# First gate weights on ACT's queue, block 0 normalised ahead of block 1's steps, its gate products in two parts

## The chip, the core and the metric

The kernel runs on one core of a Trainium2 chip. The metric is the device time of one execution in microseconds. The engines are named as in the profile: PE (TensorE, matmuls) with PEld (its weight loads), DVE (VectorE), ACT (ScalarE), POOL (GpSimd) and SP (SyncE, which issues most DMAs).

## The reference

The input x has 2048 tokens of 512 numbers. It is layer-normalised once, and the result `xn` feeds two branches whose outputs are added to x:

```python
xn = _layernorm(x)
return x + _A_ref(xn, A_wqkv, A_wo) + _B_ref(xn, B_w_in, B_w_sp, B_b_sp, B_w_out)

# A: attention, 32 heads of 16, each token sees itself and the 255 before it
scores = einsum('bhqd,bhkd->bhqk', q, k) * Dh ** (-0.5)
p = softmax(where(mask, scores, -1e9))
o = einsum('bhqk,bhkd->bhqd', p, v)  # then @ wo

# B: a gated block mixed over tokens, Fh = 688
z = gelu(einsum('bsd,df->bsf', x, w_in))          # 1376 columns
z1 = z[..., :Fh]
z2 = layernorm(z[..., Fh:])
g = einsum('ts,bsf->btf', w_sp, z2) + b_sp[None, :, None]
return einsum('bsf,fd->bsd', z1 * g, w_out)
```

## The kernel before

The 2048 tokens are 16 blocks of 128. The order on every engine is the order in which the Python program issues instructions; nothing reorders them, and each engine's queue is worked off in that order. Waits between engines are semaphores that the tile framework puts in.

Everything that the change touches lies in the first stage, which lasts to about 58 us and computes `xn`, its transpose `xnT`, the gate products `z` and some of the first q, k and v. For one block the steps are:

- a DMA loads x (`load_block` for blocks 0 to 3, `load_x` for pairs of later ones), on SP's queue;
- `stats(n)`: DVE sums (`bn_stats`, L259) and aggregates them (`bn_aggr`, L260), adds a small number to the variance (`rpow`, L119), and POOL raises it to the power -1/2 (L120);
- `norm(n)`: DVE subtracts the mean and multiplies by that power (L265), which gives `xn`;
- `transpose_x(n)`: four PE transposes into PSUM (L279), and one ACT copy from there to `xnT` (L282). From block 6 on a DMA does the transpose instead (L270);
- `do_z(n, half)`: eight matmuls (four chunks of 128 rows, each in 512 and 176 columns, L290) and a GELU on ACT (L298). Half 1 is the one that is normalised later, half 0 the gate's other factor.

The program order at the start is `warm_up(10)`, `stats(0)`, two loads, `stats(1)`, `norm(0)`, `transpose_x(0)`, `warm_up(3)`, `norm(1)`, `transpose_x(1)`, `do_z(0, 1)`, `stats(2)`, `norm(2)`, `stats(3)`, more loads, `do_z(1, 1)`, `transpose_x(2)`, `stats(4)`, `norm(3)`, `do_z(0, 0)`, and then a loop over n from 2 on that transposes block n + 1 (while that is below 6), does half 1 of block n and half 0 of block n - 1, and keeps `stats` three blocks and `norm` two blocks ahead. From n = 5 it also issues projections of q, k and v between them.

`warm_up` issues matmuls on a tile `zeros` (L251) whose results nothing reads. They run while PE would wait. The first ACT instruction is a table load with a tiny GELU (`warm`, L221). POOL prepares an identity matrix, masks (`fmask`, `esel`, L223 to L231) and one zeroed part of a weight tile (L235) before its first power. One-element memsets by DVE into a tile that a load is about to fill (L318, L332) hold that load back until DVE gets there.

The gate weights `w_in_sb` are four loads (`load_win(half, c0, c1)`, L207), all on SP's queue between the loads of x.

After this stage an order written out by hand (`ORDER`) interleaves the scores, the attention values, the token mix and the output. The change does not touch it.

Of the kernel before, what the change touches and what calls it, by code (L numbers as in the profile page):

```python
# [8 lines left out]
P = 128  # L9
BF = mybir.dt.bfloat16  # L10
F32 = mybir.dt.float32
# [8 lines left out]
FH = 688  # L20
FQ = FH // 2
NB = S_TOK // P
NDC = D // P
# [8 lines left out]
X_DMA = 6  # L32
LAST = 128
ONB = 4
N_WARM = (10, 3)

# [30 lines left out]
def kernel(  # L69
# [12 lines left out]
    nc = tc.nc  # L82
# [6 lines left out]
    xnT = pers.tile([P, NDC, S_TOK], BF, name="xnT")  # L89
# [18 lines left out]
    ps_s = ctx.enter_context(tc.tile_pool(name="ps_s", bufs=3, space=bass.MemoryType.PSUM))  # L108
    ps_y = ctx.enter_context(tc.tile_pool(name="ps_y", bufs=1, space=bass.MemoryType.PSUM))
    ps_g = ctx.enter_context(tc.tile_pool(name="ps_g", bufs=1, space=bass.MemoryType.PSUM))  # L110
    sml = ctx.enter_context(tc.tile_pool(name="sml", bufs=3))
# [5 lines left out]
    def rpow(dst, var, n):  # L117
        v = sml.tile([P, NB], F32, name="rs_v")
        nc.vector.tensor_scalar(out=v[:, :n], in0=var, scalar1=LN_EPS, scalar2=None, op0=ALU.add)  # L119
        nc.gpsimd.tensor_tensor(out=dst, in0=v[:, :n], in1=negh[:, :n], op=ALU.pow)  # L120
# [57 lines left out]
    with tc.tile_pool(name="win_pool", bufs=1) as winp, tc.tile_pool(  # L178
        name="xsp", bufs=8
    ) as xsp, tc.tile_pool(name="xnp", bufs=4) as xnp:  # L180
        w_in_sb = winp.tile([P, NDC, F], BF, name="w_in_sb")
        zeros = winp.tile([P, 512], BF, name="zeros")
        nc.vector.memset(zeros[:], 0.0)  # L183
        nc.vector.memset(fmask[:], 1.0)
        nc.vector.memset(esel[:], 1.0)
        make_identity(nc, ident[:])
        xs_tiles = {}
# [3 lines left out]
        def load_block(n):  # L191
            if n % 2 == 0:
                xs_pairs[n // 2] = xsp.tile([P, 2, D], BF, name="xs")
            xs_tiles[n] = xs_pairs[n // 2][:, n % 2, :]
            nc.sync.dma_start(out=xs_tiles[n], in_=x2[n * P : (n + 1) * P, :])
# [7 lines left out]
            for j in range(2):  # L203
                xs_tiles[2 * n2 + j] = xs[:, j, :]

        def load_win(half, c0, c1):
            nc.sync.dma_start(  # L207
                out=w_in_sb[:, c0:c1, half * FH : (half + 1) * FH],
                in_=B_w_in[c0 * P : c1 * P, half * FH : (half + 1) * FH].rearrange(
                    "(c p) f -> p c f", p=P  # L210
                ),
            )

        load_block(0)
        load_block(1)
        load_win(1, 0, 2)
        load_block(2)
        load_win(1, 2, 4)
        load_block(3)
        warm = sml.tile([P, 1], F32, name="warm")  # L220
# [3 lines left out]
            out=fmask[:], in_=fmask[:], pattern=[[-1, P]], compare_op=ALU.is_gt,  # L224
# [3 lines left out]
            out=esel[:], in_=esel[:], pattern=[[-32, 4]], compare_op=ALU.is_ge,  # L228
# [3 lines left out]
            out=esel[:], in_=esel[:], pattern=[[32, 4]], compare_op=ALU.is_ge,  # L232
# [15 lines left out]
        def warm_up(n):  # L248
            wt = ps_s.tile([P, 2, 512], F32, name="warm_t", tag="S")
            for i in range(n):  # L250
                nc.tensor.matmul(  # L251
                    wt[:, 0, :], lhsT=zeros[:, 0:P], rhs=zeros[:], start=True, stop=True
                )

        xn_tiles = {}

        def stats(n):
            st = sml.tile([P, nc.vector.BN_STATS_DIM], F32, name="st")
            nc.vector.bn_stats(out=st[:], in_=xs_tiles[n])  # L259
            nc.vector.bn_aggr(out=mvx[:, n, :], in_=st[:])  # L260
            rpow(rstdx[:, n : n + 1], mvx[:, n, 1:2], 1)

        def norm(n):
            xn = xnp.tile([P, D], BF, name="xn")
            nc.vector.tensor_scalar(  # L265
                out=xn[:], in0=xs_tiles[n], scalar1=mvx[:, n, 0:1],
                scalar2=rstdx[:, n : n + 1], op0=ALU.subtract, op1=ALU.mult,
            )
            if n >= X_DMA:
                nc.sync.dma_start_transpose(out=xnT[:, :, n * P : (n + 1) * P], in_=xn[:])  # L270
            else:
                xn_tiles[n] = xn

        def transpose_x(n):
            xn = xn_tiles.pop(n)
            pool, tag = (ps_y, "y") if n == 1 else (ps_g, "g")
            tp = pool.tile([P, NDC, P], BF, name="tp", tag=tag)
            for c in range(NDC):
                nc.tensor.transpose(  # L279
                    out=tp[:, c, :], in_=xn[:, c * P : (c + 1) * P], identity=ident[:]  # L280
                )
            nc.scalar.copy(out=xnT[:, :, n * P : (n + 1) * P], in_=tp[:])  # L282

        def do_z(n, half):
            zp2 = ps_s.tile([P, 2, 512], F32, name="zs", tag="S")
            zp = zp2[:].rearrange("p a q -> p (a q)")
            f0 = half * FH
            for c in range(NDC):
                for lo, hi in Z_RANGES:
                    nc.tensor.matmul(  # L290
                        zp[:, lo:hi],
                        lhsT=xnT[:, c, n * P : (n + 1) * P],
                        rhs=w_in_sb[:, c, f0 + lo : f0 + hi],
                        start=(c == 0),
                        stop=(c == NDC - 1),
                    )
            dst = z1_all if half == 0 else z2_all
            nc.scalar.activation(out=dst[:, n, 0:FH], in_=zp[:, 0:FH], func=ACT.Gelu_apprx_tanh)  # L298

# [14 lines left out]
        early = [(kind, 0, grp) for grp in range(3) for kind in "kqv"]  # L314

        warm_up(N_WARM[0])
        stats(0)
        nc.vector.memset(w_in_sb[0:1, 0, 0:1], 0.0)  # L318
        load_x(2)
        load_win(0, 0, 2)  # L320
        load_win(0, 2, 4)
        stats(1)
        norm(0)
        transpose_x(0)
        warm_up(N_WARM[1])
        norm(1)
        transpose_x(1)
        do_z(0, 1)
        stats(2)
        norm(2)  # L330
        stats(3)
# [3 lines left out]
        for n2 in range(4, NB // 2):  # L335
            load_x(n2)
        do_z(1, 1)
        transpose_x(2)
        stats(4)
        norm(3)  # L340
        do_z(0, 0)
        nc.vector.tensor_reduce(
            out=emask[:, 0:1], in_=esel[:], op=ALU.add, axis=mybir.AxisListType.X
        )
        nc.vector.tensor_scalar(
            out=emask[:, 1:2], in0=emask[:, 0:1], scalar1=-1.0, scalar2=1.0,
# [232 lines left out]
    def finish():  # L579
# [9 lines left out]
        out=w_out_sb[:, 0:5, :], in_=B_w_out[0:640, :].rearrange("(c p) n -> p c n", p=P)  # L589
# [52 lines left out]
```

## Time and profile before

| what | value |
|---|---|
| median of 3 runs | 265.3 us (265.15 to 265.53) |
| the profiled execution | 265.24 us |
| its span, first to last instruction | 263.5 us |
| PE busy | 256.9 us, 98% of the span |
| ACT busy | 205.5 us, 78% |
| DVE busy | 197.9 us, 75% |
| POOL busy | 122.0 us, 46% |
| x block 0, issued and landed | 0.81 and 2.95 us |
| x block 1, issued and landed | 1.27 and 3.46 us |
| first gate weights, issued and landed | 1.73 and 5.03 us |
| second gate weights, issued and landed | 2.71 and 6.38 us |
| QKV weights, issued and landed | 9.42 and 15.78 us |

A line of the timeline gives start and duration in us, engine, line, operation, what it writes and reads, shapes, how many instructions were merged, and in brackets the idle time of the engine before it and what ended that. A busy engine is one that has an instruction in flight; matmuls overlap, so two that start 0.22 us apart may each be listed with 0.38 us. The chain of waits is followed back from the last instruction, at each step to what released it.

### The profile page before, as it was taken

How to read it: one execution, taken by the hardware profiler on the slowest of the kernel's cores; microseconds unless marked ns; L12 is line 12 of the kernel's file. 1: busy time of each engine (PE TensorE's matmuls, PEld its weight loads, DVE VectorE, ACT ScalarE, POOL GpSimd, SP SyncE). 2: the span in 40 equal slices, each digit the busy share in tenths (PEclk: the TensorE clock that was granted, in tenths of full speed). 3: DMA queues.
4: the chain of work that ended last, by engine and by line, in shares of the span. 5: the costliest groups of instructions: out<-in, count | busy, mean ns of one | idle time of the engine just before them, and what ended most of it. 6: DMA issues, size and time to landing. Idle time of an engine off the chain costs nothing.

```text
span 263.5 us, 7433 instructions
## 1 busy us (share of the span) xinstructions
PE 256.9 (98%) x3166; PEld 143.4 (54%) x3199; DVE 197.9 (75%) x384; ACT 205.5 (78%) x233; POOL 122.0 (46%) x140
## 2 busy tenths in 40 slices
PE   8999999999999999999999999999999999999995
PEld 3665665654546465555565456655564454545542
DVE  5899999667786888788797778897869563786542
ACT  2777767699999999999988989988898996782000
POOL 4334446116542573768553556455468453355100
PEclk9999999999999999999999999999999999999999
DMA  7892233940505073130360322661329263636432
GB/s 215 277 301 42 42 56 68 166 161 2 109 4 112 7 105 41 43 82 13 69 82 2 80 44 41 76 51 38 82 86 179 59 132 94 140 93 151 107 85 77
DMA packets 61233, 23.83 MB, mean 90 GB/s; under 512 B 52321, under 2 KB 60689, under 8 KB 61201
## 3 DMA queue, kind: packets, MB, share of 16 engines
q1 hardware_dynamic: 60720, 23.06, 41.1%
q8 instruction: 25, 0.41, 0.7%
q10 hardware_dynamic: 432, 0.30, 0.4%
q0 software_dynamic: 48, 0.00, 0.3%
q14 instruction: 8, 0.06, 0.1%
HBM read 8.41 MB, written 2.10 MB: 40 GB/s over the span
## 4 chain that ended last, share of the span: by engine, by line
PE 97%; issue 1%; DVE 1%; DVEq 0%
PE gf L402 31%; PE zs L290 14%; PE S L496 12%; PE m L151 10%; PE o_t L549 8%; PE fo L439 8%; PE m L135 6%; PE fo L433 5%; PE warm_t L251 2%; PE tp L279 1%; DVE xnT L444 0%; DVE o_c L565 0%; DVE zeros L183 0%; DVEq L565 0%
## 5 line engine op out<-in xcount | busy, mean ns | idle before, releaser
L504 ACT ACTIVATE E<-S 128x1024 bf16<-128x1024 f32 x180 | 168.9, 1042 | 16.9 <-PE S L496 9.1
L402 PE MATMUL gf<-z_all,wspT 128*128 128x344 bf16 x512 | 95.1, 311 | 0.1
L515 POOL TENSOR_SCALAR_AFFINE_SELECT E<-E 128x1024 bf16<-128x1024 bf16 x64 | 79.3, 1262 | 31.3 <-ACT E L504 31.1
L402 PEld LDWEIGHTS <-wspT 128*128 128x128 bf16 x512 | 44.1, 98 | 35.9 <-issue 15.4
L520 DVE TENSOR_TENSOR E<-E,fmask 128x1024 bf16<-128x1024 bf16 x56 | 53.0, 973 | 2.4 <-ACT E L504 2.3
L571 POOL TENSOR_TENSOR o_norm<-o_c,rsum 128x256 bf16<-128x256 f32 x32 | 21.5, 672 | 61.9 <-DVE rsum L569 59.2
L290 PE MATMUL zs<-w_in_sb,xnT 128*128 128x512 bf16 (+1 forms) x249 | 39.1, 307 | 0.4
L496 PE MATMUL S<-q_ring,k 32*128 32x128 bf16 (+2 forms) x760 | 37.2, 267 | 0.0
L298 ACT ACTIVATE z_all<-zs 128x688 bf16<-128x688 f32 x32 | 23.8, 744 | 12.5 <-PE zs L290 12.5
L151 PE MATMUL m<-xnT,wqkv 128*128 128x512 bf16 x111 | 31.5, 380 | 1.0 <-issue 0.2
L290 PEld LDWEIGHTS <-xnT 128*128 128x128 bf16 x256 | 22.2, 98 | 14.9
L409 DVE SCALAR_TENSOR_TENSOR z_all<-gf,b_all,z_all 128x344 bf16<-128x344 f32 x32 | 18.1, 567 | 14.6 <-PE gf L402 14.6
L565 DVE STREAM_TRANSPOSE o_c<-o_t 128x512 f32<-128x512 f32 x32 | 22.3, 698 | 7.2 <-PE o_t L549 6.5
L496 PEld LDWEIGHTS <-k 32*128 32x128 bf16 x760 | 12.7, 92 | 25.9 <-issue 25.2
L444 DVE TENSOR_TENSOR xnT<-fo,xnT 128x512 bf16<-128x512 f32 (+2 forms) x17 | 11.2, 659 | 17.0 <-PE fo L439 15.3
L549 PE MATMUL o_t<-E,v 128*32 128x128 bf16 (+1 forms) x1080 | 23.4, 238 | 0.0
L439 PE MATMUL fo<-w_out_sb,uT 128*128 128x512 bf16 (+2 forms) x101 | 23.3, 366 | 0.1
L549 PEld LDWEIGHTS <-v 128*32 128x32 bf16 x1080 | 19.2, 97 | 5.1 <-issue 4.6
L171 DVE TENSOR_TENSOR k<-m,emask 128x1024 bf16<-128x1024 f32 x13 | 15.8, 1218 | 3.1 <-PE m L151 3.0
L120 POOL TENSOR_TENSOR rstdx<-rs_v,negh 128x1 f32<-128x1 f32 x16 | 10.2, 640 | 17.0 <-DVE rs_v L119 14.5
L151 PEld LDWEIGHTS <-wqkv 128*128 128x128 bf16 x128 | 11.7, 98 | 11.6 <-issue 1.7
L135 PE MATMUL m<-wqkv,xnT 128*128 128x128 bf16 x256 | 16.9, 219 | 0.2 <-DVE o_c L565 0.2
(51 smaller groups left out, 174.6 us busy)
## 6 DMA issues: line engine op xcount, KB each, us to landing
xnT<-in_A_x_dram SPq DMA_DIRECT2D x4, 512.0 KB, 4.6
out_dram<-xnT SPq DMA_DIRECT2D x13, 128.0 KB, 1.8
xs<-in_A_x_dram SPq DMA_DIRECT2D x6, 256.0 KB, 6.8
wqkv<-in_A_wqkv_dram SPq DMA_DIRECT2D x1, 1536.0 KB, 6.4
w_in_sb<-in_B_w_in_dram SPq DMA_DIRECT2D x4, 344.0 KB, 4.2
w_out_sb<-in_B_w_out_dram SPq DMA_DIRECT2D x1, 640.0 KB, 6.1
xs<-in_A_x_dram SPq DMA_DIRECT2D x4, 128.0 KB, 2.7
wo_sb<-in_A_wo_dram SPq DMA_DIRECT2D x1, 512.0 KB, 4.9
```

Of the source, the lines that this page charges most:

```text
L135: nc.tensor.matmul(m[:, j * P : (j + 1) * P], lhsT=xnT[:, c, n * P : (n + 1) * P], rhs=wqkv[:, c, 2 * D + G * P : 2 * D + (G + 1) * P], st ...
L151: nc.tensor.matmul(m, lhsT=wqkv[:, c, w0 : w0 + P], rhs=xnT[:, c, grp * 512 : (grp + 1) * 512], start=(c == 0), stop=(c == NDC - 1),)
L290: nc.tensor.matmul(zp[:, lo:hi], lhsT=xnT[:, c, n * P : (n + 1) * P], rhs=w_in_sb[:, c, f0 + lo : f0 + hi], start=(c == 0), stop=(c == NDC ...
L298: nc.scalar.activation(out=dst[:, n, 0:FH], in_=zp[:, 0:FH], func=ACT.Gelu_apprx_tanh)
L402: nc.tensor.matmul(gf[:, 0:FQ], lhsT=wsp_tiles[n][:, c, :], rhs=z2_all[:, c, lo : lo + FQ], start=(c == 0), stop=(c == NB - 1),)
L439: nc.tensor.matmul(fo[:, c0:c1], lhsT=uT_tiles[n][:, c, :], rhs=w_out_sb[:, c, c0:c1], start=False, stop=(c == NFC - 1),)
L496: nc.tensor.matmul(S[:, h2, j * P : (j + w) * P], lhsT=k_t[(G, kb // 4)][32 * s : 32 * s + 32, e, (kb % 4) * P : (kb % 4 + 1) * P], rhs=q_ ...
L504: nc.scalar.activation(out=E[:, j : j + 3 : 2, 0:nb, :].rearrange("p h b c -> p h (b c)"), in_=tiles[pr][:, :, 0 : nb * P], func=ACT.Exp, ...
L515: nc.gpsimd.affine_select(out=E[:, :, j, :], in_=E[:, :, j, :], pattern=[[0, 8], [1, P]], compare_op=ALU.is_ge, fill=0.0, base=0, channel_ ...
L520: nc.vector.tensor_tensor(out=E[:, :, j, :], in0=E[:, :, j, :], in1=fmask[:].unsqueeze(1).to_broadcast([P, 8, P]), op=ALU.mult,)
L549: nc.tensor.matmul(T[32 * s : 32 * s + 32, e, j * P : (j + l) * P], lhsT=v_t[(G, kb // 4)][:, kb % 4, s, e : e + 2, :].rearrange("p a d -> ...
L565: nc.vector.transpose(out=C[:, 0 : 32 * DH], in_=Tb)
```

## The change

There are six edits, all at the start:

- `load_win` takes a queue, and the first load of the gate weights (half 1, chunks 0 and 1) goes to ACT's queue, ahead of ACT's table load. A one-element memset of DVE into its target comes before it.
- The dummy matmuls read a constant one that exists from the start, in place of a tile that DVE zeroes. The second group has two, not three.
- `sums(n)` is the first instruction of `stats(n)`, split off, so that it can be issued alone. Block 1's sums stay ahead of `norm(0)`; its aggregate, add and power come after `norm(0)`, `transpose_x(0)` and the second dummies.
- The copy of block 0's transposes is cut in two: ACT copies chunks 0 and 1, DVE copies 2 and 3.
- `do_z(0, 1)` is issued as chunks 0 and 1, then `transpose_x(1)`, then chunks 2 and 3.
- `norm(3)` comes after block 4's sums alone, and the rest of `stats(4)` after `norm(3)`.

```diff
-N_WARM = (10, 3)
+N_WARM = (10, 2)
...
-        zeros = winp.tile([P, 512], BF, name="zeros")
-        nc.vector.memset(zeros[:], 0.0)
+        ones_w = nc.const_aps.tensor(1.0, [P, P], BF)
+        ones_m = nc.const_aps.tensor(1.0, [P, 512], BF)
...
-        def load_win(half, c0, c1):
-            nc.sync.dma_start(
+        def load_win(half, c0, c1, queue=nc.sync):
+            queue.dma_start(
...
         load_block(0)
         load_block(1)
-        load_win(1, 0, 2)
+        nc.vector.memset(w_in_sb[0:1, 0, FH : FH + 1], 0.0)
+        load_win(1, 0, 2, nc.scalar)
         load_block(2)
...
-                    wt[:, 0, :], lhsT=zeros[:, 0:P], rhs=zeros[:], start=True, stop=True
+                    wt[:, 0, :], lhsT=ones_w, rhs=ones_m, start=True, stop=True
...
+        st_tiles = {}
+
+        def sums(n):
+            st_tiles[n] = sml.tile([P, nc.vector.BN_STATS_DIM], F32, name="st")
+            nc.vector.bn_stats(out=st_tiles[n][:], in_=xs_tiles[n])
+
         def stats(n):
-            st = sml.tile([P, nc.vector.BN_STATS_DIM], F32, name="st")
-            nc.vector.bn_stats(out=st[:], in_=xs_tiles[n])
+            if n not in st_tiles:
+                sums(n)
+            st = st_tiles.pop(n)
             nc.vector.bn_aggr(out=mvx[:, n, :], in_=st[:])
...
-            nc.scalar.copy(out=xnT[:, :, n * P : (n + 1) * P], in_=tp[:])
-
-        def do_z(n, half):
-            zp2 = ps_s.tile([P, 2, 512], F32, name="zs", tag="S")
-            zp = zp2[:].rearrange("p a q -> p (a q)")
+            dst = xnT[:, :, n * P : (n + 1) * P]
+            if n == 0:
+                nc.scalar.copy(out=dst[:, 0:2, :], in_=tp[:, 0:2, :])
+                nc.vector.tensor_copy(out=dst[:, 2:4, :], in_=tp[:, 2:4, :])
+            else:
+                nc.scalar.copy(out=dst, in_=tp[:])
+
+        zp_open = {}
+
+        def do_z(n, half, c0=0, c1=NDC):
+            if c0 == 0:
+                zp_open[n] = ps_s.tile([P, 2, 512], F32, name="zs", tag="S")
+            zp = zp_open[n][:].rearrange("p a q -> p (a q)")
             f0 = half * FH
-            for c in range(NDC):
+            for c in range(c0, c1):
...
+            if c1 < NDC:
+                return
             dst = z1_all if half == 0 else z2_all
...
-        stats(1)
+        sums(1)
         norm(0)
         transpose_x(0)
         warm_up(N_WARM[1])
+        stats(1)
         norm(1)
+        do_z(0, 1, 0, 2)
         transpose_x(1)
-        do_z(0, 1)
+        do_z(0, 1, 2, NDC)
         stats(2)
...
         transpose_x(2)
+        sums(4)
+        norm(3)
         stats(4)
-        norm(3)
         do_z(0, 0)
```

## The prediction

> **What bounds the kernel now.** I read the page's chain of waits first, then the same chain in order of time at the start of the span, then the timeline of the first 14 us on every engine, because every edit lies there.
>
> ```profile
> span 263.5 us, 7433 instructions
> ...
> PE 97%; issue 1%; DVE 1%; DVEq 0%
> ```
>
> TensorE is 97% of the chain that ends last. The idle times before its matmuls show why: after 11 us the largest in the whole timeline is 0.19 us. Nothing downstream can absorb a delay or give a gain back, so whatever TensorE loses or wins before it settles into block 2's products is lost or won at the end. The chain at the start:
>
> ```profile
> 1.26 4.45 PE warm_t L251 x10
> 5.71 0.43 PE tp L279 x4
> 6.13 0.72 PE warm_t L251 x3
> 6.85 0.22 PE tp L279 x4
> 7.08 2.33 PE zs L290 x16
> 9.41 0.22 PE tp L279 x4
> 9.63 1.17 PE zs L290 x8
> 10.80 0.37 PE tp L279 x4
> ```
>
> TensorE never stops here, but the first three rows are fill: the dummy matmuls cover the time until block 0 and block 1 are normalised. Real work without a break starts with the four transposes of block 1. Only the last row holds a stall (0.37 us for transposes that take 0.22 us, for block 3's normalised tile). What feeds TensorE is one serial chain on VectorE and GpSimd, in the timeline:
>
> ```profile
> 2.98 0.69 DVE L259 BATCH_NORM_STATS2 st<-xs 128x6 f32<-128x512 bf16 x1 [1.62 <-DMA xs<-in_A_x_dram]
> ...
> 4.16 0.56 POOL L120 TENSOR_TENSOR rstdx<-rs_v,negh 128x1 f32<-128x1 f32 x1 [0.87 <-DVE w_in_sb L318]
> ...
> 5.01 0.41 DVE L265 TENSOR_SCALAR xn<-xs,mvx,rstdx 128x512 bf16<-128x512 bf16 x1
> ...
> 5.87 0.41 DVE L265 TENSOR_SCALAR xn<-xs,mvx,rstdx 128x512 bf16<-128x512 bf16 x1 [0.46 <-POOL rstdx L120]
> ...
> 6.17 0.59 ACT L282 COPY xnT<-tp 128x512 bf16<-128x512 bf16 x1 [3.87 <-PE tp L279]
> ...
> 6.92 0.18 DVE L260 BATCH_NORM_AGGREGATE mvx<-st 128x2 f32<-128x6 f32 x1
> ...
> 7.95 0.41 DVE L265 TENSOR_SCALAR xn<-xs,mvx,rstdx 128x512 bf16<-128x512 bf16 x1 [0.66 <-POOL rstdx L120]
> ```
>
> Blocks 0 and 1 are normalised at 5.01 and 5.87, 0.86 apart, because block 1's power on GpSimd (5.17) runs while block 0 is normalised. Block 2 shows the undisturbed cost: from its aggregate (6.92) to its normalising (7.95) is 1.03 us.
>
> **Part one, block 0 ahead of block 1's steps.** Block 1's aggregate and add leave the place before block 0's normalising. That now starts when its power ends, 4.16 + 0.56 + 0.02 = 4.74, so 0.27 us earlier. Its transposes follow 0.49 later as before (5.01 to 5.50): 5.23. The dummies are out of the way, since they need no zeroed tile any more; the constant one they read now is set by GpSimd at 0.36, before the start barrier that lets ScalarE and GpSimd go at 0.80. They start about 0.84 instead of 1.26, ten at the 0.43 spacing of the timeline, done at 5.1.
>
> **Part two, the split copy.** In the changed kernel as built, VectorE's half of block 0's copy waits for a semaphore of ScalarE, not of TensorE: it runs behind ScalarE's half. VectorE works in order, and behind this copy are queued block 1's aggregate, add and normalising; GpSimd's power for block 1 waits for that add, and TensorE's transposes of block 1 for the normalising. So block 1's steps, which ran beside block 0's, come after block 0's whole trip:
>
> - ScalarE's half starts 0.67 after the transposes (5.50 to 6.17): 5.90. Its length is not in the trace; 744 ns at 688 columns and 586 at 512 make 0.9 ns a column, so 0.36 (bounds 0.20, its one-column row, and 0.59): 6.26.
> - VectorE's half: 0.69 for a 512-column PSUM cast and 0.29 for a 128-column add out of PSUM make 0.42 for 256, less the 0.08 by which VectorE starts its next instruction ahead (bounds 0.2 and 0.69): the aggregate starts at 6.63.
> - Plus block 2's 1.03: block 1 is normalised at 7.66, where it was 5.87.
>
> TensorE's first four products of block 0 fill only 0.58 us of this (half of 1.17). The dummy that was dropped lies in the same hole: even two at the slow spacing end at 6.5, the products by 7.1 at full clock or 7.7 at the slow one. If block 1 came early the dummies would cost 0.2; here they cost nothing.
>
> **What is late next.** Block 1's transposes at 7.66 + 0.46 (10.31 to 10.77 for block 3) = 8.12. Their copy starts 0.42 later (6.69 to 7.11) and takes 0.59: 9.13, so block 1's products start near 9.2; they started at 8.08. That is 1.1 us. VectorE then runs block 2 (2.08 after block 1, 5.87 to 7.95) at 9.74, in time for its transposes at 9.2 + 1.17 = 10.37. Block 3 is not in time. It followed block 2 by 2.36 (7.95 to 10.31); the edit that lets only block 4's sums stand before it makes that 2.07 (sums 9.30 + 0.69, power done at 10.00). So 9.74 + 2.07 = 11.81, and transposes at 12.27, where TensorE is free at 11.76 and where they stood at 10.77. The delay is 1.50 us. Block 4 then has cover: normalised near 13.7, plus 0.46 is 14.2, needed at 12.27 + 2.57 = 14.84.
>
> The loads behind these steps move too. The fence for the QKV weights (9.31) waits about 1.8 us longer; they landed at 15.8 and were first used at 19.6, and both ends shift by nearly the same.
>
> **Part three, weights through ACT's queue.** SP's later loads issue about 0.46 earlier (one issue, 1.73 to 2.19) and none of them was waited for. ScalarE pays: it waits for VectorE's new fence (about 1.13), issues for about 0.43, and only then loads its table (1.28) and runs its warm-up (0.20), ending near 3.1 instead of 2.3. GpSimd's two small selects and the 0.53 us memset stand behind that warm-up; they end near 4.09, and block 0's power is wanted at 4.16. Taken at nothing, with 0.07 us of cover; past that every bit is paid by all blocks.
>
> The 344 KB now start near 2.2 us, beside the first two blocks of x.
>
> ```profile
> 2.00:3.00 1.00, 1.00 (x4) 0.35 (x3) 0.03 (x1) 0.29 (x2) 0.57 (x3) 1.00 0.96 247
> ```
>
> This is the window from 2 to 3 us: busy time of TensorE, its weight loads, VectorE, ScalarE and GpSimd, then the granted clock, the DMA engines' share and GB/s. At 0.96 they are full already. Block 0 landed at 2.95 and opens the chain; block 1 landed at 3.46 and has until 3.98. A gain is excluded: neither load is issued sooner. The upper bound is block 1 sharing all its time: 3.46 - 2.29 = 1.17 us becomes up to twice that, 4.6 us, 0.6 too late; an even share for the part in which the weights are there gives 0 to 0.35. I take 0.2, nearer to the lower end because block 0's packets were mostly out by 2.45. The Trainium skill ("DMA: Bandwidth & Descriptors", issuing engines are not separate DMA queues) says that DMAs of different engines share the same 16 DMA engines and interleave, so that spreading them saves issue time alone; by it this delay is above zero, and by independent queues it would be zero and the sum 0.2 us less.
>
> **Sum.** 1.50 + 0.20 = 1.70 us on the profiled execution's own 265.24 (span 263.5 and 1.74 around it; the median of the runs is 265.3): 266.9 us. With the lower bounds (halves about 0.15 shorter each, no contention, and the clock up before block 0's transposes, whose 0.67 to the copy then becomes the 0.42 of block 1) the delay is 0.95: 266.2. With VectorE's copy at its upper bound (+0.27) and contention at 0.35 it is 2.1: 267.4.
>
> **Rivals.**
> - Faster: the reorder wins and the wait behind the copy is hidden. Block 0's products start at 6.36 instead of 6.91, block 3's stall goes: 0.55 + 0.14 = 0.69, 264.6 us. It needs block 1 normalised by about 6.4, and VectorE's order speaks against it by 1.2 us. Chance 0.04.
> - No change to be measured (0.2%, 0.53 us either way): most of the delay is absorbed by early x or cheap copies. Needs both halves and the power to shrink well under their rows. 0.03.
> - Slower still, by GpSimd: if ScalarE's issue and table load end 0.1 to 0.5 later than reckoned, block 0's power is late by that less 0.07; 267.3 to 267.6. It decides from an issue that ends after 1.70. 0.12.
> - The clock falls back: TensorE idles from about 7 to 8.1. The dummies of before ran at the slow 0.43 spacing from 1.26 to about 6.1; a second such spell of 4.9 us at half speed costs 2.4: 269.3. Against it: a 1.1 us hole is short beside 4.9. 0.03. The Trainium skill ("TensorE: Matmul & The Clock Gate", Part 1) closes the gate only after a whole idle window of about 3.4 us; by it, this doesn't happen.
>
> The forecast itself has 0.78, with 266.2 to 267.4. The range adds the GpSimd case: 266.1 to 267.6. Faster 0.04, within 0.2% 0.03, slower 0.93.
>
> **What would show it.** VectorE's copy starting after ScalarE's half ends; block 1's aggregate behind it near 6.6 and its normalising near 7.7; an idle stretch of about a microsecond on TensorE before block 1's transposes; a second near 12 before block 3's; from there TensorE's rows as before, 1.5 to 1.9 us later. Block 1 normalised before 6.5 would make the forecast wrong, and block 0 normalised after 5.1 would put a share on loads or GpSimd.

## The result, and the profile after

The changed kernel takes 267.15 us (median of 5 runs, 266.83 to 267.5), the kernel before in the same series 265.48 us (265.15 to 265.77). The ratio is 1.0062, with a 95% interval of 1.0048 to 1.0076: slower by 1.67 us. The profiled execution is the one of 267.15 us (span 265.4 us), 1.91 us above the profiled one of before (265.24 us). Forecast was 266.9 us.

The engines' share of the chain of waits, from the page of the changed kernel:

```profile
PE 93%; DVE 2%; DMA 1%; issue 1%; POOL 1%; SPq 0%; ACT 0%; DVEq 0%
```

TensorE carried 97% of the chain before. The lost share has gone to a stretch at the start, which the chain in order of time spells out (start, length, what):

```profile
1.27 3.67 DMA xs<-in_A_x_dram
...
4.96 0.69 DVE st L262
5.66 0.32 DVE xn L273
...
6.03 0.41 PE tp L287 x4
...
6.46 0.38 ACT xnT L292
...
6.87 0.29 DVE xnT L293
7.16 0.10 DVE mvx L268
...
8.11 0.41 DVE xn L273
...
12.28 0.42 DVE xn L273
...
12.75 0.40 PE tp L287 x4
```

Before, this stretch was TensorE's own: dummies to 5.71, then real work with one stall. Now the chain runs through every other engine until 12.75, block 3's transposes. Two things in it are new. It begins with block 1's load of x, landed at 4.94 (before: 3.46). And it goes through both halves of block 0's copy (6.46 and 6.87) ahead of block 1's aggregate. TensorE's idle times say the same, in the timeline:

```profile
6.03 0.40 PE L287 MATMUL tp<-ident,xn 128*128 128x128 bf16 x4 [0.76 <-DVE xn L273]
8.58 0.40 PE L287 MATMUL tp<-ident,xn 128*128 128x128 bf16 x4 [0.93 <-DVE xn L273]
12.75 0.40 PE L287 MATMUL tp<-ident,xn 128*128 128x128 bf16 x4 [0.36 <-DVE xn L273]
```

Block 3's transposes stood at 10.77 before, so they are 1.98 us late. Everything after them follows at that distance: TensorE's last matmul starts at 261.99, where it started at 260.01.

The late x is the surprise. The DMA queues between 2.50 and 3.25 us, of before first and then of the changed kernel (q1 is SP's queue, q10 ACT's; packets, MB, share of the 16 DMA engines):

```profile
DMA packets 185, 0.18 MB, mean 245 GB/s; under 512 B 21, under 2 KB 185, under 8 KB 185
...
q1 hardware_dynamic: 185, 0.18, 97.5%
```

```profile
DMA packets 76, 0.09 MB, mean 119 GB/s; under 512 B 8, under 2 KB 76, under 8 KB 76
...
q10 hardware_dynamic: 56, 0.08, 57.6%
q1 hardware_dynamic: 20, 0.01, 9.9%
```

SP's queue, which carries block 1 of x, falls from 185 packets to 20, and the 16 engines together move half as much. The 185 of before also hold 45 packets of the weights, which went by SP's queue there; of x itself (packets of 1024 bytes) 119 went before and 12 in the changed kernel. The weights do not merely take a share: their first packets are slow. In the DMA records single weight packets take up to 0.70 us (0.06 us later on), and x nearly stands still meanwhile. That x's packets wait behind them on the same engines would explain it but isn't shown, as the records don't say which engine moved a packet. Before, the weights started as slowly (up to 0.59 us), but behind both blocks of x on the same queue. From 3.25 us on the engines are full again in the changed kernel and packets of the two queues alternate, too late for block 1. The weights landed at 5.14 us (before: 5.03), so the earlier issue won nothing for them either.

### The profile page after: what moved, and what is told of

It is laid out like the page before. It is cut to its first block, busy times and chain, and to the rows that moved or that the text cites. A ratio compares the mean times of both kernels' runs of the same rounds, so it can differ in the third digit from the quotient of the medians.

```text
span 265.4 us, 7432 instructions
## 1 busy us (share of the span) xinstructions
PE 257.1 (97%) x3165; PEld 142.9 (54%) x3198; DVE 197.9 (75%) x385; ACT 205.4 (77%) x233; POOL 121.7 (46%) x140
## 4 chain that ended last, share of the span: by engine, by line
PE 93%; DVE 2%; DMA 1%; issue 1%; POOL 1%; SPq 0%; ACT 0%; DVEq 0%
PE gf L423 31%; PE zs L306 13%; PE S L517 12%; PE m L151 10%; PE o_t L570 8%; PE fo L460 8%; PE m L135 6%; PE fo L454 5%; DMA xs<-in_A_x_dram 1%; DVE st L262 1%; POOL rstdx L120 1%; DVE xn L273 1%; PE tp L287 0%; DVE xnT L465 0%; DVE o_c L586 0%
```

## The experiments

Each kernel was timed beside the kernel before. Theory A in the expectations is the forecast's mechanism with a higher price on the load: block 1's steps wait for its x and then for block 0's copy. Theory G is that idle stretches on TensorE cost clock. The other rivals are in the texts. Diffs are against the changed kernel unless said otherwise. "Start shift" is how much later than before the first-stage rows stand once they follow at a constant distance (before: block 3's transposes at 10.77, block 4's at 13.34); block 3's own time is given where it helps.

### e1: first weights back on SP's queue

```diff
-        nc.vector.memset(w_in_sb[0:1, 0, FH : FH + 1], 0.0)
-        load_win(1, 0, 2, nc.scalar)
+        load_win(1, 0, 2)
```

> The changed kernel with the first gate weights back on SP's queue; the rest of the change stays. Theory A (two costs in series on VectorE's chain: block 1's x lands 1.5 us later because the weights share the DMA engines, which moves block 0's normalising from 4.74 to 5.58, and block 1's aggregate and add stand behind the copy): block 1's x lands near 3.5 again, block 0 is normalised near 4.75, block 1 near 7.5, block 3's transposes start near 12.2 (12.75 in the changed kernel, 10.77 before): 0.3 to 0.6 us below the changed kernel, about 1.2 above before. Rival B (the loads are the whole cost): back at before, within 0.2 us. Rival C (the order behind the copy is the whole cost): no difference from the changed kernel.

Measured: 266.36 us (266.12 to 266.56), before 265.37; ratio 1.0034 (1.0021 to 1.0047). The chain in order of time, block 0's half copies and what follows:

```profile
5.93 0.38 ACT xnT L291
...
6.34 0.29 DVE xnT L292
...
7.58 0.41 DVE xn L272
...
12.21 0.40 PE tp L286 x4
```

Block 1 of x landed at 3.37, block 0 was normalised at 4.86. The start shift is 1.44 us: the wait behind the copy alone, and within 0.06 of the forecast's 12.27 for block 3. So the load is worth 1.97 - 1.44 = 0.53 us in the shift and 0.68 us in the medians' differences (1.67 and 0.99). Rivals B and C are both out: the time is neither that of before nor that of the changed kernel.

### e2: only the load through ACT's queue, in the kernel before

Against the kernel before:

```diff
+        nc.vector.memset(fmask[:], 1.0)
+        nc.vector.memset(w_in_sb[0:1, 0, FH : FH + 1], 0.0)
         nc.vector.memset(zeros[:], 0.0)
-        nc.vector.memset(fmask[:], 1.0)
...
-        load_win(1, 0, 2)
+        load_win(1, 0, 2, nc.scalar)
```

Two memsets now stand ahead of the zeros that the dummies read, so the dummies start at 1.44 us, where it was 1.26.

> The kernel before with only its first gate weights on ACT's queue (and the one-element fence memset for that). Theory A: block 1's x lands near 4.9, its sums start there, and since in this order aggregate and add of block 1 also stand ahead of block 0's normalising, that comes near 6.0 instead of 5.01; every later row moves by the same, 0.9 to 1.0 us above before. Rival B (the loads are the whole cost): as slow as the changed kernel, 1.6 to 1.9 above before. Rival C: no difference from before.

Measured: 266.08 us (265.8 to 267.59, 10 runs), ratio 1.0036 (1.0021 to 1.005): +0.71. Two of the ten took 267.49 and 267.59, and the first of these is the profiled one. Its timeline shows why:

```profile
7.23 1.49 PE L252 MATMUL warm_t<-zeros 128*128 128x512 bf16 x3
...
8.51 0.63 PE L280 MATMUL tp<-ident,xn 128*128 128x128 bf16 x4
```

Three dummies take 1.49 us where they took 0.93 before, and the transposes 0.63 where full speed makes it 0.39: TensorE ran at half speed until 10.17 us, where it came to full speed at 6.15 before. It had idled for 0.94 us before block 0's transposes, as block 1 of x landed at 5.33 and its sums stand ahead of block 0's normalising. So the load alone costs about 0.7 us in the median: more than the 0.2 I took, less than the 0.9 to 1.0 expected here (e5 has the reason), and far from Rival B's 1.6. In some executions a late clock comes on top.

### e3: block 1's aggregate, add and power issued ahead of block 0's transposes and copy

```diff
         norm(0)
+        stats(1)
         transpose_x(0)
         warm_up(N_WARM[1])
-        stats(1)
         norm(1)
```

> The changed kernel with block 1's aggregate and add issued before block 0's transposes, so that VectorE's half copy stands behind them and only block 1's normalising behind the copy. Theory A: block 1 is normalised near 7.1 (8.11 in the changed kernel), block 3's transposes start near 11.7, 1.0 us below the changed kernel and 0.8 to 0.9 above before. Rival D (what costs is the wait of VectorE's half for ScalarE's half, whatever stands behind it): the halves stay in series, so less than 0.3 us below the changed kernel. Rival B: no difference from the changed kernel.

Measured: 266.2 us (266.07 to 266.5), ratio 1.0032 (1.002 to 1.0044); start shift 1.04. The load is left as in the changed kernel, the copy too. VectorE's rows:

```profile
6.00 0.17 DVE L268 BATCH_NORM_AGGREGATE mvx<-st 128x2 f32<-128x6 f32 x1
...
6.98 0.29 DVE L293 COPY xnT<-tp 128x256 bf16<-128x256 bf16 x1 [0.62 <-ACT xnT L292]
...
7.19 0.40 DVE L273 TENSOR_SCALAR xn<-xs,mvx,rstdx 128x512 bf16<-128x512 bf16 x1
```

With the power running beside the copy, block 1 is normalised at 7.19 instead of 8.11, although x is as late as ever. 0.93 us of the start shift is gone, where Rival D allowed less than 0.3. The order of VectorE's queue is a cause by itself.

### e4: block 0's copy whole on ACT

```diff
-            if n == 0:
-                nc.scalar.copy(out=dst[:, 0:2, :], in_=tp[:, 0:2, :])
-                nc.vector.tensor_copy(out=dst[:, 2:4, :], in_=tp[:, 2:4, :])
-            else:
-                nc.scalar.copy(out=dst, in_=tp[:])
+            nc.scalar.copy(out=dst, in_=tp[:])
```

> The changed kernel with the whole of block 0's copy on ScalarE; VectorE has no part in it. Theory A: block 1's aggregate follows block 0's normalising at once (5.9), block 1 is normalised near 6.95, block 3's transposes start near 11.6, 1.1 to 1.2 us below the changed kernel and 0.7 to 0.8 above before (the late load stays). Rival B (loads alone): no difference from the changed kernel. Rival E (block 0's first products are what sets the time, and they start later with a whole copy): slower than the changed kernel by 0.2.

Measured: 266.23 us (265.77 to 267.23, 10 runs), ratio 1.0034 (1.0023 to 1.0045); start shift 1.04, block 1 normalised at 7.18. The same as e3 by another road: it is VectorE's half copy, standing ahead of block 1's steps, that holds them. Two of the ten executions took 267.1 and 267.23; a late clock as in e2 would fit, but no trace of them was kept.

### e5: both undone, the load on SP and the copy on ACT

The edits of e1 and e4 together.

> The changed kernel with both suspected costs taken away: the first gate weights back on SP's queue, and the whole of block 0's copy on ScalarE. Theory A: block 0 is normalised near 4.8, block 1 near 6.2, block 3's transposes start near 10.8, as before (10.77): within 0.2 us of before, either way. If something else in the change costs (the dummies' constant, the products in two parts), it stays 0.3 us or more above before. Rival F (with block 1's aggregate and add still behind block 0's normalising, the rest of the change gains): 0.3 us or more below before.

Measured: 264.99 us (264.85 to 265.4, 11 runs), before 265.29 (23 runs); ratio 0.9989 (0.9981 to 0.9998). The slowdown is gone. TensorE's chain at the start:

```profile
0.84 4.42 PE warm_t L251 x10
...
5.94 0.60 ACT xnT L290
...
6.58 0.76 PE zs L301 x4
7.34 0.24 PE tp L286 x4
```

The start shift is +0.10, so the edits that are left (the early dummies, the order of normalising, the products in two parts, block 4's sums) bring nothing at the start that block 3's transposes would keep. The median is 0.30 us below before, which is Rival F's number, but not for its reason: the 0.3 us come from elsewhere. In the kernel before and in the changed one TensorE waits in the middle for a transpose of VectorE, as in this row of the changed kernel:

```profile
86.58 1.05 PE L135 MATMUL m<-wqkv,xnT 128*128 128x128 bf16 x16 [0.20 <-DVE o_c L586]
```

With what follows it the wait is worth 0.29 us: e5's last matmul starts 0.19 us earlier than that of before (259.82 and 260.01), after a start shift of +0.10. The wait is in the profiles of before, after, e3, e4, e6, e7, e9 and e11 and missing in e1, e2, e5, e8 and e10. This is also part of why e1's median is 0.99 and not 1.44 above before, and e8's 0.74 and not 1.07. What decides it was not found.

### e6: two small edits alone, in the kernel before

Against the kernel before, with `sums` split off as in the change:

```diff
-N_WARM = (10, 3)
+N_WARM = (10, 2)
...
-        stats(4)
-        norm(3)
+        sums(4)
+        norm(3)
+        stats(4)
```

> The kernel before with two edits of the change alone: two dummies in the second group instead of three, and block 3 normalised after block 4's sums alone. Theory A: nothing is put behind a copy and no load moves; block 0's products start near 6.8 instead of 6.91 and block 3's transposes near 10.53 instead of 10.77: 0.2 us below before, at the edge of what can be measured. If the order ahead of block 3's transposes doesn't matter: no difference from before.

Measured: 265.14 us (265.01 to 265.54, 11 runs), ratio 0.9994 (0.9985 to 1.0003): not to be told from no change. In the profiled execution (265.44 us) block 3's transposes stand at 10.97. The chain names a load there (issued at 4.69, landed at 10.35: a part of the other half's weights), not block 3's normalising.

### e7: block 0's products in one piece

```diff
-        do_z(0, 1, 0, 2)
         transpose_x(1)
-        do_z(0, 1, 2, NDC)
+        do_z(0, 1)
```

> The changed kernel with block 0's products in one piece behind block 1's transposes, as before. Theory A (block 3's normalised tile sets TensorE's place, through VectorE): the first four products leave the hole at 6.9, block 1's products start near 9.97 instead of 9.66, and block 3's transposes still near 12.75: no difference from the changed kernel, within 0.15 us. Rival E (TensorE's own work at the start sets the time): 0.3 us above the changed kernel.

A miss: 268.67 us (267.06 to 270.4, 6 runs), ratio 1.0125 (1.009 to 1.016). The profiled execution is the fastest of the six, and its timeline has the expected place for block 3 (12.67), with a longer hole ahead of block 1's transposes:

```profile
5.96 0.40 PE L287 MATMUL tp<-ident,xn 128*128 128x128 bf16 x4 [1.31 <-DVE xn L273]
...
8.51 0.40 PE L287 MATMUL tp<-ident,xn 128*128 128x128 bf16 x4 [1.72 <-DVE xn L273]
```

The two executions at 267.06 and 267.3 had a mean granted clock of 1.00; the others 0.994 (268.36 and 268.99), 0.986 (269.84) and 0.985 (270.4). All five timed executions of the changed kernel had 0.998 or more. So the products that the change puts into the hole (0.76 us of them at 6.89), though they move no row of the chain, seem to keep the clock up there; e9 tests that. The other runs of this series (e5, e6, e8) had 0.998 or more in every execution.

### e8: e2 with three more dummies

Against e2:

```diff
-N_WARM = (10, 3)
+N_WARM = (13, 3)
```

> The run with the ACT queue alone, with 13 dummies in the first group instead of 10, so that TensorE has no hole before block 0's transposes. The profiled execution of that run had its matmuls at 0.43 us spacing until 10 us, and it took 267.49 where the median was 266.08. Theory G (the hole from 5.7 to 6.8 lets the clock come up a whole window late in some executions): no execution above 266.8, median near 266.0. Rival H (the late executions come from the load's landing alone): some executions stay near 267.5.

Measured: 266.03 us (265.92 to 266.63, 5 runs), ratio 1.0032 (1.002 to 1.0044). TensorE has no hole ahead of block 0's transposes (6.54), and none of the five executions is late. Two late in ten against none in five is thin, but the median (+0.74) and the start shift (+1.07) again price the load alone, this time with the clock up in time.

### e9: e7 with nine dummies where it had two

Against e7:

```diff
-N_WARM = (10, 2)
+N_WARM = (10, 9)
```

> The changed kernel with block 0's products in one piece (which alone gave 267.06 to 270.4) and nine dummies in the second group instead of two, so that TensorE has work from block 0's transposes to about 8.2 us. Theory G (in the run without them, the empty stretch from 6.8 to 8.5 makes the clock fall or come up late in most executions): all executions near the changed kernel, 266.9 to 267.6. Rival I (the products in one piece cost by their place in the queue, whatever fills the hole): median above 268 again.

Measured: 267.3 us (267.02 to 268.37, 6 runs), ratio 1.0074 (1.006 to 1.0088). TensorE's rows:

```profile
6.60 2.13 PE L252 MATMUL warm_t<-const-bfloat16-1.0 128*128 128x512 bf16 x9
8.92 0.40 PE L287 MATMUL tp<-ident,xn 128*128 128x128 bf16 x4 [0.19 <-DVE xn L273]
```

The hole of e7 is filled with work that nothing reads, and 1.4 us come back; five of six executions are within 267.02 to 267.48. The one at 268.37 (clock 0.998) may come from the hole before block 0's transposes, which is still there (1.86 us); that wasn't tested.

### e10: e5, with the sums of later blocks in VectorE's waits

Against e5:

```diff
         stats(1)
+        sums(2)
         norm(1)
-        do_z(0, 1, 0, 2)
         transpose_x(1)
-        do_z(0, 1, 2, NDC)
+        do_z(0, 1)
         stats(2)
+        sums(3)
         norm(2)
```

> The run with ScalarE's whole copy and the weights on SP, further with the sums of blocks 2 and 3 ahead of the normalising of blocks 1 and 2 (in VectorE's waits for GpSimd), and block 0's products in one piece behind block 1's transposes. Theory A: block 3 is normalised near 9.3 instead of 10.36 and no longer late, block 1's products start near 8.05 instead of 8.24, block 3's transposes near 10.7 instead of 10.89: 0.1 to 0.2 us below that run. If the landing of the x blocks holds the sums back, no difference.

Measured: 265.03 us (264.75 to 265.54, 12 runs), ratio 0.9984 (0.9975 to 0.9992). It is 0.16% below the kernel before and isn't to be told from e5. Block 2's transposes start at 9.44, e5's at 9.41. Block 3 is normalised at 9.96, where it was 10.31 before, and its transposes wait all the same, until 11.18, for products that wait for weights:

```profile
4.68 5.87 DMA w_in_sb<-in_B_w_in_dram
...
10.60 0.74 PE zs L301 x4
11.34 0.22 PE tp L286 x4
```

This is the load that e6's chain named. Once VectorE's chain is shortened, that landing is what comes next. The start shift is +0.39; the time is no longer because the wait of 0.29 us described at e5 is missing.

### e11: the load on ACT's queue, held until block 0's sums have started

```diff
-        nc.vector.memset(w_in_sb[0:1, 0, FH : FH + 1], 0.0)
-        load_win(1, 0, 2, nc.scalar)
...
         warm_up(N_WARM[0])
+        sums(0)
+        nc.vector.memset(w_in_sb[0:1, 0, FH : FH + 1], 0.0)
+        load_win(1, 0, 2, nc.scalar)
         stats(0)
```

> The changed kernel with the first gate weights still on ACT's queue, but issued behind the warm-up and held back until block 0's sums are taken (near 3.7 us), so that they are not in flight beside blocks 0 and 1 of x. Theory A: block 1's x lands near 3.4, block 0 is normalised near 4.75, block 1 near 7.5, block 3's transposes start near 12.2, as with the weights on SP: about 0.5 us below the changed kernel; the weights land later, near 7, into the hole before block 1's transposes. Rival J (ACT's queue itself delays the loads of x, whenever it is used): block 1's x late as in the changed kernel, no difference from it.

A miss: 270.8 us (269.61 to 272.51, 6 runs), ratio 1.0206 (1.0178 to 1.0234). The side of x does what holding the load was to do: block 1's sums start at 3.99, straight after block 0's steps, block 0 is normalised at 4.75 and block 1 at 7.30. So Rival J is out. But the weights, issued at 3.72 beside what SP had issued before, now come last:

```profile
9.13 1.31 PE L304 MATMUL zs<-w_in_sb,xnT 128*128 128x512 bf16 x4 [3.08 <-DMA w_in_sb<-in_B_w_in_dram]
10.23 0.63 PE L285 MATMUL tp<-ident,xn 128*128 128x128 bf16 x4
```

Four products take 1.31 us (0.76 in the changed kernel). Windows of 2 us (TensorE, its weight loads, VectorE, ScalarE, GpSimd, granted clock, DMA share, GB/s) show the clock itself:

```profile
8.00:10.00 2.00, 0.87 (x3) 0.40 (x3) 1.27 (x5) 0.00 (x0) 0.55 (x1) 0.51 0.90 320
...
12.00:14.00 2.00, 2.00 (x9) 0.93 (x7) 1.90 (x8) 0.74 (x1) 1.06 (x2) 0.50 0.80 237
```

The clock falls at 8.04 us, 1.99 us into the hole of 3.08 us, and TensorE runs at half speed until 14.87 us. Block 3's transposes stand at 15.87, 5.1 us late. The profiled execution loses a further 1.6 us in one place: TensorE idles for 1.54 us before 62.28 us, for a cast of VectorE that stands behind a load of 4 KB (the bias `b_bf`), which landed 14.4 us after its issue where it took 6.0 before. The waiting weights, not x, are the main price of this version.

## Why the prediction was right

The direction, the engine and the mechanism hold, and the total is within the range. Two terms were wrong in size, and partly offset each other, so the closeness of the total is partly luck.

**The wait behind the copy: right, 1.50 forecast, 1.44 measured** (e1, where the load is out of the way). Its steps there and in the forecast: block 0 normalised at 4.86 (4.74), ScalarE's half copy at 5.93 (5.90) for 0.38 (0.36), VectorE's half behind it for 0.29 (0.42, the one size that was clearly off), block 1's aggregate at 6.54 (6.63), its normalising at 7.58 (7.66), block 2's at 9.66 (9.74), block 3's at 11.75 (11.81). VectorE's copy does wait for ScalarE's, and e3 and e4 each take about 0.9 us off the changed kernel by freeing block 1's steps from it. The stall ahead of block 3's transposes, and the cover for block 4, came as worked out.

**The load: the step that failed.** I let block 1 of x be late by "0 to 0.35" and took 0.2, with an upper bound of 4.6 us for its landing. It landed at 4.94, beyond that bound, because I divided bandwidth and the trace shows a near stall: 12 packets of x where 119 went. In the shift this cost 0.53 us (1.97 against e1's 1.44); e2 and e8 give 0.71 and 0.74 in the median for the load alone. The reason given, that block 0's packets "were mostly out by 2.45", was beside the point: block 0 landed at 2.99 (2.95 before), and it was block 1 that stood still. The rule of the Trainium skill ("DMA: Bandwidth & Descriptors", issuing engines are not separate DMA queues) agrees with this trace in that the packets of the two queues alternate and together fill the engines from 3.25 us on (share 1.02). The load of the other queue paid.

**Why the total still came near.** Block 1's sums were 0.85 us late to start (4.96, VectorE idle for 0.85), so block 0 was normalised at 5.58, 0.84 after the forecast's 4.74 and past the 5.1 that the prediction had named as the sign of a share on loads or GpSimd. Of this 0.24 came back because the first transposes ran at full speed and ScalarE followed them after 0.43 instead of 0.67, and 0.13 through VectorE's shorter half copy. Block 3's transposes came at 12.75, where the working with its 0.20 for the load has 12.47. Against the forecast delay of 1.70 the profiled executions differ by 1.91 and the medians by 1.67.

**The two terms don't add up.** Load alone 1.07 (e8), copy alone 1.44 (e1), both 1.97 and not 2.51. The rows account for the gap. Block 1's sums are 0.86 later than in e1 (4.96 and 4.10), in e8 1.06 later than before: 0.20. In e1 block 0's normalising waits for GpSimd's power after those sums, in the changed kernel it follows them at once: 0.14. And from there ScalarE's half copy follows 0.19 sooner, as the first transposes run at full speed.

**The rivals.** The faster one needed block 1 normalised by 6.4; it was 8.11, and even e5, at 6.19, wins nothing at the start. GpSimd was no problem: its memset ended at 4.14, and block 0's power started at 4.20, straight after VectorE's add. The clock did not fall in the changed kernel, with its holes of 0.76 and 0.93 us; but this rival was further from safe than 0.03 says. Without the split products, in four of six executions, it costs 1.3 to 3.3 us (e7), and the argument that a hole of 1.1 us is short beside 4.9 doesn't stand beside e7, whose profiled execution has holes of 1.31 and 1.72. The Trainium skill ("TensorE: Matmul & The Clock Gate", Part 1) has the gate close after a whole idle window of about 3.4 us. These runs differ from that: e11's clock fell 1.99 us after TensorE's last matmul, and TensorE had been busy for 1.21 of the 3.41 us before the fall.

**Edits valued at nothing.** The early dummies and block 4's sums are worth nothing that shows (e5, e6). The split products, taken as fill, are worth 1.7 us in the median (e7 is 3.38 above before, the changed kernel 1.67).

## What to carry to other kernels

A load moved to another queue isn't priced by bandwidth alone: look at which small, urgent load is in flight when it starts; here x moved 12 packets where it had moved 119 while the first packets of the new load were slow. When an engine that works in order takes over part of another's job, list what stands behind it and issue that first where the data allow it (e3 won back 0.93 us of start shift by one moved line). And before taking fill out of a hole on TensorE, or making one longer, count the clock: with early holes of 1.3 and 1.7 us, e7 lost up to 3.3 us in some executions, twice what the whole change cost.

## What the runs showed that was not expected

- The first packets of the gate weights are far slower than the rest, in every trace: up to 0.70 us for 1376 bytes in the changed kernel, 0.06 us later in the same load. In the changed kernel the 16 engines moved 119 GB/s during that spell, with 245 GB/s before in the same window, though packets of x were waiting. Why the engines stay partly idle was not found.
- TensorE reaches full speed at a different time in each profiled execution: 3.58 (e9) to 6.15 us (before), and 10.17 in that of e2. The granted clock in the windows reads 1.00 throughout that first spell, while dummies are 0.43 us apart, as the trace's clock records begin only at the rise; only the later fall in e11 shows in it (0.50).
- The clock changes at boundaries 3.41 us apart: e11's records are 3.41 us at full speed, 6.83 at half and 256.00 at full, and the first full-speed record of every other run is 256.00, 259.41 or 262.83 us long, each a whole multiple of 3.413. What counts seems to be how busy TensorE was between two boundaries. At full speed 36% busy lost it (e11, 4.63 to 8.04), 46% and 47% kept it (e9 from 3.58, e7 from 3.88); at half speed 80% gained it (e9, 0.17 to 3.58), 75% did not (e2, 3.34 to 6.75). In e7's rows 3.41 us laid across both holes (4.65 to 8.06) hold 0.83 us of work, 24%; in the changed kernel none hold less than 1.69, about half. So whether an execution of e7 loses its clock would hang on where its boundaries fall. That is inferred: no trace of a slow execution of e7 was kept.
- A copy of 128 x 256 from PSUM to bf16 takes 0.37 us on ScalarE and 0.29 us on VectorE. In e4 and e5 the whole 512 columns on ScalarE take 0.58 to 0.60 us, so that the pair in a row, with the semaphore between, takes longer (6.46 to 7.16 in the changed kernel).
